# A gated mix of two long convolutions on one core: the product of filter and v written along positions, raw v in the inverse matrix's room, the step size in the transposing matmuls, another order of calls

## The chip, the cores and the metric

The kernel runs on one core of one Trainium2 chip. The metric is the device time of an execution in microseconds. The kernel before took 270.42 us in the median of three runs (269.96 to 270.56).

A core has a matrix engine (PE, whose weight loads are listed apart as PEld), VectorE (DVE), ScalarE (ACT), GpSimd (POOL), and SyncE (SP), which here only issues DMAs. They share an SBUF of 128 partitions, and PE writes to PSUM, from which DVE or ACT must copy ("evacuate") every result.

## The reference

Sequence length 2048, 448 channels, 256 modes per channel, batch 1, everything in bf16:

```python
# a: a state space model's kernel K made from 256 complex modes, as a causal convolution
dt = exp(log_dt)
K = einsum("dn,dnl,dn->dl", Cc, exp((dt * A)[:, :, None] * l), dt * Bc).real
a = causal_conv(K, u) + u * Dskip                 # by FFT of twice the length
# b: k filtered by 4 taps, times v, convolved with ssm_k, gated by u
k_shift = sum over t in 0..3 of k_pad[:, t:t + S] * shift_k[:, 3 - t]
kv = k_shift * v
b = u * (causal_conv(ssm_k, kv) + kv * ssm_D)
# the mix
g = sigmoid((u * gate_w).sum(-1, keepdims=True))
out = g * a + (1 - g) * b
```

`causal_conv` stands for the FFTs of the reference.

## The kernel before

**Tiling.** A channel is (g, l) with g one of 4 and l one of 112; a position is (a, b) with a one of 32 and b one of 64, position 64a + b. Data in "natural" layout lies on partitions (g, a) with 64 x 112 elements (b, l) each. The 112 values of l are worked in four groups H of NC = 28, so a group is 4 x 28 = 112 channels.

**A convolution** (`conv_B`, `conv_A`) of a group is a chain of matrix products in place of FFTs. A *spread* (line 422) takes, for each of the 28 columns, the 64 values of b as the matmul's weights (`lhsT`) and multiplies by Wc, twice, 56 matmuls of 128 columns each; four evacuations. A *transform* (434) runs 32 matmuls with weights W2, four evacuations. One of the two operands is copied with its halves exchanged by eight DMAs on SP (`swapped`, 813). DVE then makes two *products* of 3584 elements (480). *Stage A* (451) runs 56 matmuls against R, four evacuations; *stage B* (462) 128 matmuls of 28 columns against G, the inverse matrix, and its two results go to an epilogue on DVE. Branch B spreads the filter ssm_k (tile sk, columns side by side) and kv; ssm_D is added to the filter's first element from the tile dB (`load_sk`, 801). Branch A spreads u and the generated K. Stage B of branch A starts with `less` (962), which subtracts branch B's result by a matmul with minus the identity.

**The tables.** K of branch A comes from a *table* T of the group (`table`, 995): phases on PE, sines and exponentials on ACT (`levels`, 530; each change between sine and exponential loads a function table, ACT_TABLE_LOAD in the profile), then a chain of DVE multiplications and additions (`tables`, 658), some additions being POOL's accumulating DMAs; PE sums over the modes (`sums`, 691) and puts the rows in order (`gather`, 543, tile RK), and the spread uses the weights WcK. Table 3 is made in two halves. Ahead of the tables `Modes.run` (718) multiplies the modes' parameters and transposes the products of B and C, c2, into the tile hold.

**The filter on k** (913 to 925): k is loaded transposed into four tiles kT (837), and 448 matmuls with diagonal weights dg write 8 PSUM rooms, on partitions (g, a) with 8 x 112 results each; a DVE multiplication (925) takes a room times v, which lies in the tile natv in the natural layout (vt), in place. So a column of kv that the spread loads as weights has its 64 values 112 elements apart.

**Rooms and order.** There are 7 SBUF slots q of 3584 elements, 4 PSUM rooms ps of 2 x 512 words, and an arena of named tiles (natv, natu, sk, TQ, TP, ET, RK, and G). The three strings SLOTS, ROOMS and SIDES say for every request which slot or room it gets and whether an evacuation runs on VectorE (V) or ScalarE (S). The functions do not issue anything: the class Order (130) records 6562 calls, and `issue` then issues them in the order that the hand-written list ORDER gives. Each engine works its instructions off in that order, so the list also sets every queue's order, SP's DMA issues included. In the profile all of them carry line 142. In the order of PLAN the work is T0 B0 B1 T1 B2 A0 T2 B3 A1 T3 A2, the four mixes, A3; ORDER interleaves it. Only A3's epilogue (972) stores the output.

Of the kernel before, what the change touches and what calls it, by code (L numbers as in the profile page):

```python
# [23 lines left out]
NQG = 4  # L24
# [18 lines left out]
    "0153244660452356221105413561200342542265346120"  # L43
)
ROOMS = (
    "01300231231021302012133123211302103213113003213200301121010223323302100020322020223203123321230021323232021310333102"
    "21110012102130031202201020010102031123321123033210013321033213312112313230110231311332233320003030113132211112000223"
    "212023230102121"
)
SIDES = (  # L50
    "SVVSSSSSVSSSSSSSSSSSSSSSSVSSSSSSSSSSSSSSSSSSSVSVSSSSSSSSSSSVSVSSSSSSSSSSVVSSSSSSSSSSSSSSSSSSSSSSSSSSSSSSSSSSVSVSSSSS"
    "SSVVVSSSSSSSSSSSSSSSSSSSSSSSSSSSSSSSSSSVVSSVSSSSSSVVSSVVSSSSVSSSSSSSSSSSSSSSSSSSSSSSSSSSVSVSVVSSSS"
)
ORDER = (
# [1032 lines left out]
```

## Time and profile before

| | |
|---|---|
| median of 3 runs (lowest, highest) | 270.42 us (269.96, 270.56) |
| the profiled execution | 270.07 us |
| its span, first instruction to last | 268.3 us |
| PE busy | 230.2 us (86%) |
| DVE busy | 225.3 us (84%) |
| ACT busy | 202.2 us (75%) |
| POOL busy | 26.5 us (10%) |
| granted PE clock, mean over the span | 0.917 |
| HBM read, written | 8.68 MB, 3.15 MB |

The profile is one execution. A row of its groups has the engine, the operation, the tiles written and read, the shape (partitions x elements) and the number of instructions, then the busy time and the mean duration of one in ns, then the engine's idle time just before such instructions and what ended it. A row of the timeline has the start and the length in us, then engine, line, operation and tiles, and how many alike follow one another. A row of a stage table has the window, its length, then for PE, PEld, DVE, ACT and POOL the busy time with the count, then the granted PE clock as a share of the full one, then the busy share of the DMA engines and GB/s.

### The profile page before, as it was taken

To read this page: it belongs to the slowest core of one execution; us is meant where nothing else is said; L and a number is where in the kernel's file an instruction comes from. 1 tells how busy PE (TensorE), PEld (TensorE's weight loads), DVE (VectorE), ACT (ScalarE), POOL (GpSimd) and SP (SyncE) were. 2 spreads that over 40 slices of the span, in tenths; PEclk is the share of its full clock that TensorE was granted. 3 is DMA by queue.
4 is the path that set the end of the run, shared out by engine and by line. 5 is a ranking of instruction groups with operands and counts; after the bars stand their busy time and mean duration, and the time that the engine had idled before them with its cause. 6 is when DMAs were issued, how large, how long until landed. Compare 5 with 4: busy or idle time off the path is not lost.

```text
span 268.3 us, 12631 instructions
## 1 busy us (share of the span) xinstructions
PE 230.2 (86%) x5735; PEld 196.7 (73%) x5735; DVE 225.3 (84%) x330; ACT 202.2 (75%) x266; POOL 26.5 (10%) x111
## 2 busy tenths in 40 slices
PE   0475885999989999899999999999999989989740
PEld 0122433799977998898798998988999968889730
DVE  7999899977959899996989998969999965867840
ACT  5899899512978999798999797899999853746300
POOL 8910002010000020100000210000220210000000
PEclk9996586599999999999999999999999968999955
DMA  6789999923791969344005815400632560240076
GB/s 135 125 242 211 203 162 157 201 59 73 136 156 28 187 119 147 72 103 107 6 2 122 157 37 114 115 5 20 135 62 37 98 148 5 55 91 2 2 155 121
DMA packets 60279, 27.58 MB, mean 103 GB/s; under 512 B 50114, under 2 KB 57666, under 8 KB 60226
## 3 DMA queue, kind: packets, MB, share of 16 engines
q1 hardware_dynamic: 53234, 19.90, 39.5%
q0 software_dynamic: 2160, 5.51, 11.8%
q10 hardware_dynamic: 4832, 1.38, 2.4%
q8 instruction: 45, 0.74, 1.2%
q14 instruction: 8, 0.07, 0.1%
HBM read 8.68 MB, written 3.15 MB: 44 GB/s over the span
## 4 chain that ended last, share of the span: by engine, by line
PE 67%; ACT 15%; DVE 8%; issue 4%; DMA 2%; SPq 0%; POOL 0%; ACTq 0%; DVEq 0%; POOLq 0%
PE ps L142 67%; ACT q L142 8%; ACT ET L142 4%; DVE G L142 3%; DVE TP L142 2%; DMA natu<-in_A_u_dram 2%; DVE RK L142 2%; ACT TP L142 1%; ACT s_W L142 1%; ACT G L142 1%; ACT RK L142 1%; ACT L142 0%; DVE ET L142 0%; SPq L142 0%; DVE gx L142 0%
## 5 line engine op out<-in xcount | busy, mean ns | idle before, releaser
L142 ACT CAST q<-ps 128x1024 bf16<-128x1024 f32 (+4 forms) x150 | 125.1, 925 | 37.4 <-PE ps L142 37.0
L142 PEld LDWEIGHTS <-q 128*128 128x128 bf16 (+3 forms) x792 | 56.3, 139 | 11.8 <-issue 8.0
L142 DVE TENSOR_TENSOR TQ<-TQ,ET 128x896 bf16<-128x896 bf16 (+2 forms) x70 | 45.7, 687 | 0.4
L142 PE MATMUL ps<-q,s_W 128*128 128x112 bf16 (+1 forms) x544 | 36.0, 217 | 6.0 <-ACT q L142 2.9
L142 PEld LDWEIGHTS <-s_W 128*128 128x128 bf16 x544 | 28.9, 101 | 10.8 <-issue 8.4
L142 DVE TENSOR_TENSOR q<-q,q 128x3584 bf16<-128x3584 bf16 (+1 forms) x22 | 32.5, 1512 | 3.1 <-ACT q L142 2.5
L142 PE MATMUL ps<-TP,TQ 128*32 128x32 bf16 x1792 | 33.6, 240 | 1.3 <-issue 1.2
L142 PEld LDWEIGHTS <-TQ 128*32 128x32 bf16 x1792 | 29.8, 154 | 6.2 <-issue 4.8
L142 PEld LDWEIGHTS <-G 128*128 128x128 bf16 x1024 | 28.5, 97 | 5.2 <-issue 3.1
L142 PE MATMUL ps<-sa_R,q 128*128 128x128 bf16 x448 | 31.9, 228 | 0.1
L142 POOL DMA_DIRECT2D TP<-TP x15 | 13.0, 876 | 188.6 <-PE ps L142 109.7
L142 PEld LDWEIGHTS <-natu 128*32 128x32 bf16 (+1 forms) x560 | 28.4, 187 | 4.3 <-issue 2.5
L142 PE MATMUL ps<-q,G 128*128 128x28 bf16 x1024 | 29.4, 176 | 0.7 <-ACT q L142 0.7
L142 DVE TENSOR_TENSOR TP<-TP,ET 128x3584 bf16<-128x3584 bf16 (+1 forms) x15 | 24.4, 1646 | 0.0
L142 PE MATMUL ps<-TP 128*128 128x512 bf16 x32 | 10.9, 505 | 10.7 <-POOL TP L142 10.3
L142 DVE CAST q<-ps 128x896 bf16<-128x896 f32 (+2 forms) x14 | 14.0, 1015 | 6.8 <-PE ps L142 6.8
L142 PE MATMUL ps<-Wc,natu 128*64 128x128 bf16 x224 | 16.3, 291 | 1.3 <-issue 1.3
L142 ACT ACTIVATE q<-ps 128x896 bf16<-128x896 f32 x16 | 13.8, 926 | 4.4 <-PE ps L142 4.3
L142 DVE TENSOR_TENSOR TQ<-TQ 128x448 bf16<-128x448 bf16 (+2 forms) x35 | 15.4, 448 | 0.4
L142 PE MATMUL ps<-q,natu 128*32 128x336 bf16 (+3 forms) x336 | 15.8, 309 | 0.0
L142 PEld LDWEIGHTS <-TP 128*128 128x128 bf16 x32 | 3.7, 121 | 16.5 <-POOL TP L142 10.3
L142 PE MATMUL ps<-q,q 128*32 128x336 bf16 (+3 forms) x112 | 15.6, 308 | 0.0
(87 smaller groups left out, 307.9 us busy)
## 6 DMA issues: line engine op xcount, KB each, us to landing
q<-q SPq DMA_DIRECT2D x64, 112.0 KB, 3.6
TP<-TP POOLq DMA_DIRECT2D x9, 448.0 KB, 5.6
sk<-in_B_ssm_k_dram SPq DMA_DIRECT2D x16, 112.0 KB, 4.3
natv<-in_B_v_dram SPq DMA_DIRECT2D x4, 448.0 KB
natu<-in_A_u_dram SPq DMA_DIRECT2D x4, 448.0 KB
TP<-TP POOLq DMA_DIRECT2D x6, 224.0 KB, 4.1
scratch<-ET SPq DMA_DIRECT2D x4, 280.0 KB
out_dram<-natv SPq DMA_DIRECT2D x8, 112.0 KB, 4.8
```

The source lines that it names most:

```text
L142: ins = f(*args, **kw)
```

## The change: where kv, raw v and the results lie, the scaling of B, and the lists

- v is loaded raw into the first 7168 elements of G's room. The product with the filter is written to natv as [112, 64], along positions, so that a column that the spread loads as weights lies side by side (`kv`).
- Branch B's results, so far written over kv in natv, go to `held_in[H]`, one contiguous block [64, 28] for each group in natv. The mix and the last epilogue write to natu, and the output is stored from there.
- `Modes.run` no longer multiplies B_re and B_im by dt (8 ACT instructions). The identity of the transposing matmuls is replaced by identity times dt (`dts`, one DVE multiplication of 112 x 448), so they scale while they transpose. They are matmuls into two f32 rooms instead of transposes into one bf16 room. The work tiles go from 8 to 6; 4 of them lie in G's room at 3584 words and 2 in TQ.
- The gate's weights come by one DMA instead of four.
- SLOTS, ROOMS, SIDES (33 instead of 27 evacuations on VectorE, among 206 instead of 214) and ORDER are new. 6552 calls are recorded instead of 6562.

```diff
-    "0153244660452356221105413561200342542265346120"
+    "0214365652544341630245362166044633152502310654"
...
 def run(self):
-        t, whole, rate, br, bi, x, y, z = self.work
+        t, whole, rate, x, y, z = self.work
...
-        self.scaled(br, "B_re", dt)
-        self.scaled(bi, "B_im", dt)
-        cr, ci = self.raw["C_re"], self.raw["C_im"]
+        br, bi, cr, ci = (self.raw[n] for n in ("B_re", "B_im", "C_re", "C_im"))
...
-        room = self.places.room()[:].rearrange("p a n -> p (a n)").bitcast(bf16)
         for i in range(2):
-            pt = room[:, 1024 * i:1024 * i + 896]
+            room = self.places.room()
             for hf in range(2):
                 for g in range(4):
-                    nc.tensor.transpose(out=pt[:, (hf * 4 + g) * 112:(hf * 4 + g + 1) * 112],
-                                        in_=self.c[i][:, g, hf * 128:(hf + 1) * 128], identity=self.ident[0:112, 0:112])
...
+                    nc.tensor.matmul(room[:, hf, g * 112:(g + 1) * 112], lhsT=self.c[i][:, g, hf * 128:(hf + 1) * 128], rhs=self.ident[:, g], start=True, stop=True)
...
-    vt = arena["natv"][:].rearrange("p (b l) -> p b l", l=112)
+    at = G[:].rearrange("p b r g a -> p (b r g a)")
+    vt = shaped(at, [64, 112])
+    kv = shaped(arena["natv"][:], [112, 64])
...
-    for g in range(4):
-        nc.sync.dma_start(gw[g * 32:(g + 1) * 32], gate_w[g * 112:(g + 1) * 112].partition_broadcast(32))
+    nc.sync.dma_start(gw[:], gate_w.rearrange("(g l) -> g l", g=4).unsqueeze(1).to_broadcast([4, 32, 112]))
...
-    modal = Modes(nc, places, raw, ident, cols, work, N5, c2, hold, evac)
+    dts = cons.carve(224)[0:112].bitcast(bf16).rearrange("p (g l) -> p g l", g=4)
+    V.tensor_tensor(out=dts, in0=ident[0:112, 0:112].unsqueeze(1).to_broadcast([112, 4, 112]), in1=dt.unsqueeze(2).to_broadcast([112, 4, 112]), op=ALU.mult)
+    modal = Modes(nc, places, raw, dts, cols, work, N5, c2, hold, evac)
...
-        o = vt[:, b0:b0 + 8].rearrange("p (i b) l -> p i (b l)", i=2)
-        V.tensor_tensor(out=o, in0=pt[:, :, 0:448], in1=o, op=ALU.mult)
+        V.tensor_tensor(out=kv[:, :, b0:b0 + 8].rearrange("p l (i b) -> p l i b", i=2), in0=pt[:, :, 0:448].rearrange("p i (b l) -> p l i b", b=4),
+                        in1=vt[:, b0:b0 + 8].rearrange("p (i b) l -> p l i b", i=2), op=ALU.mult)
...
+    held_in = [shaped(arena["natv"][:], [64, NC], at=64 * NC * H) for H in range(4)]
...
-            o = window(ug, b0, n, H).rearrange("p (i b) c -> p i b c", b=16)
+            o = held_in[H][:, b0:b0 + n].rearrange("p (i b) c -> p i b c", b=16)
...
-    less = lambda H: (minus[:], lambda b0, n: window(ug, b0, n, H))
+    less = lambda H: (minus[:], lambda b0, n: held_in[H][:, b0:b0 + n])
...
-            V.tensor_tensor(out=window(ug, b0, n, H), in0=t, in1=window(ug, b0, n, H), op=ALU.add)
+            V.tensor_tensor(out=window(uu, b0, n, H), in0=t, in1=held_in[H][:, b0:b0 + n], op=ALU.add)
...
-        X = spread_in(lambda c: vt[:, :, H * NC + c])
+        X = spread_in(lambda c: kv[:, H * NC + c, :])
...
-        V.tensor_tensor(out=o, in0=o, in1=x, op=ALU.add)
+        V.tensor_tensor(out=x, in0=o, in1=x, op=ALU.add)
```

In the new ORDER, on DVE the addition of dB into group 0's filter stands behind table 0's first large multiplication; on SP the transposed loads of k stand behind those of v; U's loads and the gate's matmuls stand earlier, as do branch A0's spread and transform; B2's spreads and B1's stages A and B stand later; the exponentials of table 1 stand on both sides of table 0's remaining sines on ACT; the second half of A2's stage B stands behind A3's stage A.

More of the change, by code (lines that the diff above doesn't have):

```diff
@@ L42 @@
 SLOTS = (
-    "0153244660452356221105413561200342542265346120"
+    "0214365652544341630245362166044633152502310654"
 )
 ROOMS = (
-    "01300231231021302012133123211302103213113003213200301121010223323302100020322020223203123321230021323232021310333102"
-    "21110012102130031202201020010102031123321123033210013321033213312112313230110231311332233320003030113132211112000223"
-    "212023230102121"
+    "31020301233213020130221213002030121220330312300132203112223221301101222032123012231331111303121132010020233210031013"
+    "11200130210201030120231211331231202021230013233013332112300103220100303223020203023223012113221023331330101121312331"
+    "0003313003131020"
 )
 SIDES = (
-    "SVVSSSSSVSSSSSSSSSSSSSSSSVSSSSSSSSSSSSSSSSSSSVSVSSSSSSSSSSSVSVSSSSSSSSSSVVSSSSSSSSSSSSSSSSSSSSSSSSSSSSSSSSSSVSVSSSSS"
-    "SSVVVSSSSSSSSSSSSSSSSSSSSSSSSSSSSSSSSSSVVSSVSSSSSSVVSSVVSSSSVSSSSSSSSSSSSSSSSSSSSSSSSSSSVSVSVVSSSS"
+    "VSVSVSSSVVSSSVVSSSSSSSSSSSSSSSSSSSSVSSVSSSSSSSSSSSSSSSSSVSSVSSSVVVSSSSSSSSVSSSSSSSVSSSSSSSSSSSSSSSSSSSSSSSSSSSSVSSSS"
+    "SSSSSSSSSSVSSSSVSVVSVSSSSSSSSSSSSVSSSSSSVSVVVVSSSSSSSVSSSSSSSSSSSSSSSSSSSSSSSSVSVSSVSSSVSS"
 )
 ORDER = (
[54 rows of a table removed]
[54 rows of a table added]
 )
@@ L742, in run @@
         mul(z, br, ci)
-        mul(bi, bi, cr)
-        V.scalar_tensor_tensor(out=c[1], in0=fl(z), scalar=-1.0, in1=fl(bi), op0=ALU.mult, op1=ALU.subtract)
-        room = self.places.room()[:].rearrange("p a n -> p (a n)").bitcast(bf16)
+        mul(x, bi, cr)
+        V.scalar_tensor_tensor(out=c[1], in0=fl(z), scalar=-1.0, in1=fl(x), op0=ALU.mult, op1=ALU.subtract)
         for i in range(2):
-            pt = room[:, 1024 * i:1024 * i + 896]
+            room = self.places.room()
             for hf in range(2):
                 for g in range(4):
-                    nc.tensor.transpose(out=pt[:, (hf * 4 + g) * 112:(hf * 4 + g + 1) * 112],
-                                        in_=self.c[i][:, g, hf * 128:(hf + 1) * 128], identity=self.ident[0:112, 0:112])
-            self.evac(self.hold[:, :, i].rearrange("p h (q w) -> p q h w", q=8), pt.rearrange("p (q h w) -> p q h w", q=8, h=4))
+                    nc.tensor.matmul(room[:, hf, g * 112:(g + 1) * 112], lhsT=self.c[i][:, g, hf * 128:(hf + 1) * 128], rhs=self.ident[:, g], start=True, stop=True)
+            self.evac(self.hold[:, :, i].rearrange("p h (f q w) -> p f q h w", f=2, q=4), room[:, :, 0:448].rearrange("p f (q h w) -> p f q h w", q=4, h=4))
 @with_exitstack
@@ L879, in body @@
     nc.sync.dma_start(scratch[:].rearrange("(x w) n -> x w n", w=32)[:, 28:32], spare.unsqueeze(1).to_broadcast([20, 4, 1024]))
-    at = G[:].rearrange("p b r g a -> p (b r g a)")
-    work = [shaped(at, [4, 256], i32 if i == 1 else f32, at=1024 * i)[0:112] for i in range(8)]
+    work = [shaped(at if i < 4 else arena["TQ"][:], [4, 256], i32 if i == 1 else f32, at=1024 * i + (3584 if i < 4 else -2048))[0:112] for i in range(6)]
     N5 = shaped(arena["ET"][:], [5, 1024])[0:112]
     c2 = [shaped(arena["RK"][:], [4, 256], at=1024 * i)[0:112] for i in range(2)]
-    modal = Modes(nc, places, raw, ident, cols, work, N5, c2, hold, evac)
+    dts = cons.carve(224)[0:112].bitcast(bf16).rearrange("p (g l) -> p g l", g=4)
+    V.tensor_tensor(out=dts, in0=ident[0:112, 0:112].unsqueeze(1).to_broadcast([112, 4, 112]), in1=dt.unsqueeze(2).to_broadcast([112, 4, 112]), op=ALU.mult)
+    modal = Modes(nc, places, raw, dts, cols, work, N5, c2, hold, evac)
     modal.run()
@@ L929, in body @@
         nc.sync.dma_start(uu[g * 32:(g + 1) * 32], u4[g])
-    ug = vt
+    held_in = [shaped(arena["natv"][:], [64, NC], at=64 * NC * H) for H in range(4)]
     gwt = qt([112, 32])
@@ L955, in epilogue_B, with held @@
         return consume
-    def held(t, H):
+    def held(H):
         def consume(b0, n, pt):
-            evac(window(t, b0, n, H).rearrange("p (i b) c -> p i b c", b=16), pt.rearrange("p i (b c) -> p i b c", b=16))
+            evac(held_in[H][:, b0:b0 + n].rearrange("p (i b) c -> p i b c", b=16), pt.rearrange("p i (b c) -> p i b c", b=16))
         return consume
-    less = lambda H: (minus[:], lambda b0, n: window(ug, b0, n, H))
+    less = lambda H: (minus[:], lambda b0, n: held_in[H][:, b0:b0 + n])
     def store(b0, n):
         for g in range(4):
-            dmae[g % 2].dma_start(out4[g][:, b0:b0 + n, :], ug[g * 32:(g + 1) * 32, b0:b0 + n, :])
+            dmae[g % 2].dma_start(out4[g][:, b0:b0 + n, :], uu[g * 32:(g + 1) * 32, b0:b0 + n, :])
     def gated(dst, b0, n, pt):
@@ L990, in conv_B @@
         K, S = swapped(K)
-        X = spread_in(lambda c: vt[:, :, H * NC + c])
+        X = spread_in(lambda c: kv[:, H * NC + c, :])
         transform(nc, places, W2, X, evac)
-        conv(products(nc, K, S, X), epilogue_B(H) if H < NQG - 1 else held(ug, H))
+        conv(products(nc, K, S, X), epilogue_B(H) if H < NQG - 1 else held(H))
     def table(H):
@@ L1034, in mix @@
     def mix(H):
-        o, x = window(ug, 0, 64, H), window(uu, 0, 64, H)
+        o, x = held_in[H], window(uu, 0, 64, H)
         if H == NQG - 1:
```

108 rows, old and new, of the table ORDER are left out of this document.

## The prediction

> **What bounds the kernel now.** I read the head of the page first, then the chain of work that ended last, then a table of busy time by stage.
>
> ```profile
> span 268.3 us, 12631 instructions
> PE 230.2 (86%) x5735; PEld 196.7 (73%) x5735; DVE 225.3 (84%) x330; ACT 202.2 (75%) x266; POOL 26.5 (10%) x111
> PE 67%; ACT 15%; DVE 8%; issue 4%; DMA 2%; SPq 0%; POOL 0%; ACTq 0%; DVEq 0%; POOLq 0%
> ```
>
> TensorE carries two thirds of the chain, but VectorE has only 5 us less work. The stages below are cut where the filter's matmuls begin (48.3), where the first sums of tables 0, 1, 2 and 3 (both halves) begin (73.7, 123.7, 173.7, 208.3, 227.7) and where the last stage A ends (251.4). The columns are length, then busy time of PE, PEld, DVE, ACT, POOL with counts, the granted clock, and DMA.
>
> ```profile
> 0.00:48.30 48.30, 27.97 (x166) 13.74 (x166) 44.68 (x99) 41.76 (x60) 14.79 (x96) 0.80 1.01 176
> 48.30:73.70 25.40, 25.19 (x628) 23.08 (x626) 21.61 (x23) 11.72 (x15) 0.86 (x1) 0.91 0.60 114
> 73.70:123.70 50.00, 47.14 (x1291) 43.32 (x1289) 42.78 (x49) 44.74 (x58) 2.56 (x3) 1.00 0.66 118
> 123.70:173.70 50.00, 50.00 (x1350) 43.92 (x1347) 46.40 (x51) 44.49 (x58) 2.56 (x3) 1.00 0.38 80
> 173.70:208.30 34.60, 34.32 (x986) 31.97 (x985) 31.87 (x56) 32.70 (x44) 2.87 (x4) 1.00 0.26 50
> 208.30:227.70 19.40, 18.12 (x533) 15.89 (x531) 13.82 (x27) 11.62 (x15) 2.90 (x4) 0.82 0.42 87
> 227.70:251.40 23.70, 22.30 (x665) 20.58 (x666) 18.35 (x22) 14.10 (x19) 0.00 (x0) 1.00 0.19 43
> 251.40:268.30 16.90, 5.21 (x136) 4.18 (x133) 5.77 (x10) 1.03 (x2) 0.00 (x0) 0.59 0.57 110
> ...
> 0.00:72.90 72.90, 52.35 (x782) 36.15 (x782) 65.48 (x121) 52.68 (x73) 15.65 (x97) 0.84 0.87 155
> 72.90:120.90 48.00, 45.14 (x1222) 41.31 (x1220) 43.26 (x49) 43.33 (x58) 2.56 (x3) 1.00 0.66 117
> ```
>
> Up to 48.3 PE is idle for 20 us while DVE and ACT build constants: DVE sets that stage, with 3.6 us idle. From 48.3 to 251.4 PE is idle for 6.0 us in all. From 123.7 on it is plainly the bound, DVE standing idle for 17.3 of 127.7 us (127.7 less 46.40, 31.87, 13.82 and 18.35). The last two rows are cut where DVE ends the tables 0 and 1.
>
> **The change part by part.** *The product along positions.* B's spread of v loads 64 columns of v as weights, 224 times; so far they lie 224 bytes apart. The spread of the filter has the same shape with its columns side by side.
>
> ```profile
> L142 PE MATMUL ps<-Wc,natv 128*64 128x128 bf16 x224 | 14.9, 283 | 0.0
> L142 PE MATMUL ps<-Wc,sk 128*64 128x128 bf16 x224 | 9.7, 240 | 0.6 <-ACT TP L142 0.3 <-ACT q L142 0.2
> ...
> 96.48 1.06 PE L142 MATMUL ps<-Wc,sk 128*64 128x128 bf16 x32
> 97.50 1.17 PE L142 MATMUL ps<-Wc,natv 128*64 128x128 bf16 x16
> ...
> 98.91 2.10 PE L142 MATMUL ps<-Wc,natv 128*64 128x128 bf16 x32
> 100.94 1.77 PE L142 MATMUL ps<-q,G 128*128 128x28 bf16 x64
> 102.64 1.49 PE L142 MATMUL ps<-WcK,RK 128*64 128x128 bf16 x40
> 104.06 0.96 PE L142 MATMUL ps<-q,s_W 128*128 128x112 bf16 x16
> 104.89 0.28 PE L142 MATMUL ps<-q,G 128*128 128x28 bf16 x5
> ...
> 138.08 3.71 PE L142 MATMUL ps<-sa_R,q 128*128 128x128 bf16 x56
> 141.72 0.47 PE L142 MATMUL ps<-Wc,sk 128*64 128x128 bf16 x10
> ```
>
> From start to start, 32 strided ones take 2.03 us (63 ns each) and 32 contiguous ones 1.02 (32 ns). So the change takes 31.5 ns off each, 7.1 us for 224; the busy sums give 5.2 (14.9 less 9.7) as the other end. I take 7.1, because PE is the bound where most of them stand. The same rows give the other paces I need: 27 ns a matmul of stage B (1.70 over 64), 52 of a transform (0.83 over 16), 65 of stage A (3.64 over 56).
>
> The product itself now reads PSUM and raw v across positions and writes runs of four elements. No row shows that operation.
>
> ```profile
> L142 DVE TENSOR_TENSOR natv<-ps,natv 128x896 bf16<-128x896 f32 x8 | 8.5, 1086 | 3.7 <-PE ps L142 3.7
> L142 DVE CAST RK<-ps 128x896 bf16<-128x896 f32 x1 | 1.1, 1092 | 2.0 <-PE ps L142 2.0
> L142 DVE TENSOR_TENSOR q<-q,TP 128x1344 bf16<-128x1344 bf16 x1 | 1.5, 1548 | 0.0
> L142 DVE TENSOR_SCALAR G<-q,TP 112x256 f32<-112x256 bf16 x3 | 1.1, 373 | 0.0
> L142 DVE CAST q<-ps 128x1024 bf16<-128x1024 f32 x3 | 3.7, 1220 | 0.5 <-PE ps L142 0.5
> L142 DVE TENSOR_TENSOR q<-q,q 128x3584 bf16<-128x3584 bf16 x14 | 27.9, 2020 | 2.9 <-ACT q L142 2.5 <-DMA q<-q 0.4
> L142 ACT ACTIVATE G<-q,TP 112x256 f32<-112x256 bf16 x13 | 5.7, 495 | 0.3 <-DVE TP L142 0.3
> L142 ACT ACT_TABLE_LOAD x10 | 12.8, 1283 | 2.8 <-issue 1.5 <-PEq L1071 1.2
> ```
>
> The gather's copy (RK) reads PSUM strided and writes the same runs of four in 1092 ns, so 1.09 us is the lower end and my value: no change. The upper end adds a strided SBUF read at the pace of the diagonals' build (1548 over 1344, 1.15 ns an element, 1.03 us for 896): 2.1 us, or 8.2 us more for eight.
>
> *Step size in the transposing matmuls.* Eight ACT multiplies go (495 ns each, 4.0 us). DVE gains one build of 448 elements (0.5 us at 1.15 ns). The sixteen matmuls stay; the copies out read f32 of the same size.
>
> *One load of the gate weights for four.* SP issues three small DMAs less; their users come 40 us later, behind U's loads, so I cost this at nothing.
>
> *The order.* The list of copies moves work from ACT to DVE. Read with the row durations (1.22 and 1.09 us a copy of 1024 or 896, 0.4 to 0.7 for the small ones), 20 us go to DVE and 17 come back, so with the new build DVE's total rises by about 4 us, to 229. ACT's falls by 8.
>
> *The start.* Four things move here.
>
> ```profile
> 30.38 0.27 DVE L142 TENSOR_TENSOR sk<-sk,dB 128x28 bf16<-128x28 bf16 x1
> ...
> 41.60 3.95 DVE L142 TENSOR_TENSOR TP<-TP,ET 128x3584 bf16<-128x3584 bf16 x2
> ...
> 48.34 0.62 PE L142 MATMUL ps<-q,natu 128*32 128x448 bf16 x3
> ...
> 64.50 1.53 PE L142 MATMUL ps<-Wc,sk 128*64 128x128 bf16 x48
> 75.17 1.28 ACT L142 ACT_TABLE_LOAD   x1
> ...
> 76.47 0.98 ACT L142 ACTIVATE ET<-ps 128x448 bf16<-128x448 int16 x2
> ```
>
> First, the add of dB into the filter, at 30.38 so far, goes behind table 0's chain up to its first large multiply (41.60 plus 2.0), the scale of R and about 1.8 us that are new to DVE (the build, a cast, a negation), so it comes near 45.5. The first K spread waits for it, then its four copies on ACT with one exponential of 0.9 between them and the four transforms: the filter's matmuls begin near 52 instead of 48.34. Second, table 1's first exponentials now stand on both sides of table 0's sines. That is two table loads more, 2.6 us at 1283 ns, and uses up most of what the eight multiplies leave. Third, SP issues the four transposed loads of k behind raw v and the scratch writes; they then land some 5 us ahead of 52, and the filter waits for them only if they slip by more. Fourth, raw v now shares G's room, so G's lower fills wait for its DMAs; these are issued before 30 and the fills stand behind 35 on DVE, where table 0's next step would wait behind them. I cost both at nothing.
>
> On the table loads a page speaks against the change: the Trainium skill, "ScalarE: Activation LUTs", section "What ACT_TABLE_LOAD costs", adds a drain of about 1.38 us to the load itself, 2.66 us a switch. By that, two more switches would be an estimated 5.3 us. The trace disagrees: the load at 75.17 lasts 1.28 us and the next activation starts 20 ns after it.
>
> *Table 0 and 1.* Until table 0 ends, DVE has about 2.9 us more to do (a late cast, the build, copies) and still the 3.6 us of idle time of the start; its waits for the filter, 3.8 us so far, fall mostly away, since the eight products now stand later. I take 2.5 us late: 75.4 for 72.9. Until table 1 ends it then has less: the two products of B1 (2 times 2.02), one epilogue and copies of 5.4 us go behind, and the gate weights' spread (2.0) and copies of some 1.7 come ahead, 5.7 us net. So 43.3 less 5.7 is 37.6 of work, with 4.5 of idle time for 4.7: table 1 ends at 117.5 for 120.9.
>
> *Behind it.* By the list, PE has less done when table 1's sums begin: B2's two spreads (56 at 32 and 56 at 63 ns, 5.3 us), 72 transform matmuls (3.7), B1's stage A (3.6) and stage B (128 at 27, 3.5) go behind them, 16.1 us; the gate's 112 matmuls, 24 transform matmuls and four of table 2 come ahead, about 5.5. So 10.6 us move behind. PE had 124.7 us busy from 123.7 to 251.4 and 3.0 idle. From it go the strided loads of B2 and B3 (112 at 31.5, 3.5 us) and A2's second half of stage B, which now fills the wait after stage A:
>
> ```profile
> 246.62 0.54 PE L142 MATMUL ps<-natv,minus 128*128 128x448 bf16 x2
> ...
> 248.61 2.99 PE L142 MATMUL ps<-sa_R,q 128*128 128x128 bf16 x44
> ```
>
> That is 2.0 us. 124.7 plus 10.6 less 3.5 less 2.0 is 129.8. The stage from 208.3 to 227.7 ran at a clock of 0.82, 18 per cent of 19.4 us, 3.5 us lost; the PE pause behind it comes at another place of the new list, and I count half, 1.7, as gone. Stage A ends at 117.5 + 129.8 + 3.0 - 1.7 = 248.6 for 251.4. The tail then holds A2's epilogue and the last mix on DVE (1.09 each) inside the same 16.9 us; I add 0.3.
>
> **The sum.** 268.3 - 2.8 + 0.3 = 265.8 us of span. The profiled execution took 270.07, 1.77 around its span and 0.35 under the median of 270.42. The change of -2.5 put on that median gives **267.9 us**.
>
> **The rivals.** *DVE takes over as the bound* (slower). Behind table 1 DVE had 110.4 us of work and gets 6.9 more, the 4 of the total and the 2.8 that table 1 no longer holds. It may then idle for 13.8 of PE's 131.1 us; so far it idled for 17.3. If each of those waits stays, stage A ends at 117.5 + 117.3 + 17.3 = 252.1, and the time is 271.4. It decides as soon as DVE idles for more than 13.8 us between 117.5 and stage A's end. For it speaks that DVE is busy for 46.40 of 50 us behind 123.7; against it, that its waits were for PE, which now has less to do.
>
> *The late start is not won back* (slower). If the products cost their upper end, or the filter comes at 56 instead of 52, table 1 ends at 121.5 or later. PE has 129.8 us behind that, so 4 us more: 271.9, and up to 276 with both. Against it, the gather's copy at 1092 ns.
>
> *No change.* The strided loads may be hidden: PE's 16 matmuls at 63 ns take 1.0 us, an ACT copy of their 1024 elements takes about as long, so where spreads stand alone ACT paces them. Without the 3.5 us and with the clock's dip as long as before, stage A ends at 253.8 for 251.4, and with the tail's 0.3 the time is 270.42 + 2.7, 273.1; with table 1 ending 2.5 us earlier than I take, as it would if its start were not late, 270.6.
>
> *All of it counts.* If DVE idles only for 2 us between the tables and the dip goes wholly, stage A ends 4.2 us earlier: 263.7.
>
> **How the numbers follow.** Forecast 0.42, its own range 265 to 269.8; all of it 0.11; no change 0.08; DVE bound 0.22; late start 0.17. From 0.2 per cent, 0.54 us, a measurement of this kernel can tell a difference. Faster: 0.42 and 0.11, 0.53. Slower: 0.22 and 0.17, 0.39. Within: 0.08. The range, 263 to 274.5, leaves out the far ends of the late start and of the gain.
>
> **What would show it.** Right: spreads of v at about 32 ns a matmul, products at 1.09 us, filter matmuls from about 52, twelve table loads, table 1's first sums near 117.5, PE without gaps behind them, stage A ending near 248.6. Wrong: products above 1.5 us, table 1's sums after 120, DVE ahead of PE in the chain behind them, or a clock below 1.00 for more than one stretch between the filter and the tail.

## The result, and the profile after

The changed kernel takes 279.59 us in the median of four runs (278.36 to 280.20), the kernel before on the same chip 270.31: a ratio of 1.0338, interval 1.0300 to 1.0377. It is slower by 9.3 us; the forecast was 2.5 us faster.

One thing belongs to the reading of this time: the four fills of G's lower half ran from 36.73 to 39.5 us, behind v's loads into that room and ahead of the first product, so the product's second operand is by then G's numbers and not v. Every instruction has the shape and place that the change gives it. The runs rows, early_db, tail and prices below have the same order of fills.

The head of the page:

```profile
span 278.0 us, 12624 instructions
PE 222.2 (80%) x5735; PEld 192.2 (69%) x5735; DVE 234.6 (84%) x337; ACT 198.9 (72%) x254; POOL 27.4 (10%) x111
PE 55%; ACT 13%; DVE 11%; issue 5%; SPq 5%; POOL 4%; DMA 3%; ACTq 0%; DVEq 0%; POOLq 0%
```

PE has 8 us less to do, and yet the span is 9.7 us longer; DVE has 9.3 us more, where the forecast added 4. The table of busy time by stage has the columns of the prediction's. It is cut where the filter's matmuls begin (54.25), at the first spread of the product (75.02), at table 0's and table 1's first sums (82.07, 124.9) and at the end of the last stage A (259.3); the last row but two is the stretch ahead of that end:

```profile
0.00:54.25 54.25, 28.00 (x170) 14.25 (x170) 49.04 (x107) 40.33 (x51) 15.65 (x96) 0.79 0.86 161
54.25:75.02 20.77, 14.03 (x450) 13.38 (x450) 19.53 (x17) 2.53 (x3) 0.86 (x1) 0.91 0.77 139
75.02:82.07 7.05, 6.26 (x114) 5.68 (x115) 6.08 (x6) 5.28 (x7) 0.00 (x0) 0.73 1.34 166
82.07:124.88 42.81, 39.64 (x1118) 35.52 (x1117) 37.85 (x44) 36.85 (x49) 2.56 (x3) 0.92 0.36 65
...
239.30:259.30 20.00, 17.61 (x478) 16.38 (x469) 16.84 (x20) 9.78 (x14) 0.00 (x0) 0.91 0.18 39
...
124.90:259.30 134.40, 128.17 (x3691) 117.89 (x3691) 116.18 (x158) 112.14 (x144) 8.29 (x11) 0.99 0.37 75
259.30:278.00 18.70, 6.08 (x198) 5.43 (x196) 5.89 (x11) 1.74 (x2) 0.00 (x0) 0.69 0.54 100
```

The second row is the one to look at. In 20.8 us of filter, VectorE works 19.53, ScalarE 2.53, and PE 14.03: the stage that PE set before now belongs to VectorE. The groups by shape say with what:

```profile
L142 DVE TENSOR_TENSOR q<-q,q 128x3584 bf16<-128x3584 bf16 x14 | 27.8, 2018 | 3.7 <-DMA q<-q 3.6
L142 DVE TENSOR_TENSOR natv<-ps,G 128x896 bf16<-128x896 f32 x8 | 14.8, 1896 | 1.2 <-PE ps L142 1.2
...
L142 PE MATMUL ps<-Wc,natv 128*64 128x128 bf16 x224 | 9.8, 256 | 6.4 <-DVE natv L142 6.3
L142 PE MATMUL ps<-Wc,sk 128*64 128x128 bf16 x224 | 9.7, 248 | 5.7 <-DVE sk L142 5.5 <-ACT q L142 0.3
L142 ACT ACT_TABLE_LOAD x12 | 15.4, 1283 | 2.0 <-issue 1.8
```

The product costs 1.90 us for 1.09. The spread of the product now costs what the spread of the filter does, 9.8 us for 14.9, as the change means it to. Both spreads show a wait of some 6 us (the last column), where there was 0.0 and 0.6: for the first product's rows, and for the addition of dB into the filter. Table 0's sums come 8.3 us later than before (82.07 for 73.73), table 1's 1.2 (124.88 for 123.73), the end of stage A 7.7 (259.3 for 251.6).

### The profile page after: what moved, and what is told of

Its sections match the earlier page's. It is cut to its first block, busy times and chain, and to the rows that moved or that the text cites. A ratio compares the mean times of both kernels' runs of the same rounds, so it can differ in the third digit from the quotient of the medians.

```text
span 278.0 us, 12624 instructions
## 1 busy us (share of the span) xinstructions
PE 222.2 (80%) x5735; PEld 192.2 (69%) x5735; DVE 234.6 (84%) x337; ACT 198.9 (72%) x254; POOL 27.4 (10%) x111
## 4 chain that ended last, share of the span: by engine, by line
PE 55%; ACT 13%; DVE 11%; issue 5%; SPq 5%; POOL 4%; DMA 3%; ACTq 0%; DVEq 0%; POOLq 0%
PE ps L142 55%; ACT q L142 10%; SPq L142 5%; DVE natv L142 4%; POOL TP L142 3%; DVE TQ L142 2%; DMA sk<-in_B_ssm_k_dram 1%; DMA scratch<-ET 1%; ACT RK L142 1%; DVE natu L142 1%; DVE G L142 1%; DMA q<-q 1%; DVE RK L142 1%; ACT TP L142 1%; DVE TP L142 1%
## 5 line engine op out<-in xcount | busy, mean ns | idle before, releaser
L142 ACT CAST q<-ps 128x1024 bf16<-128x1024 f32 (+4 forms) x145 | 122.2, 935 | 41.2 <-PE ps L142 40.3
L142 PEld LDWEIGHTS <-q 128*128 128x128 bf16 (+3 forms) x792 | 57.1, 140 | 15.8 <-issue 10.7
L142 PE MATMUL ps<-q,s_W 128*128 128x112 bf16 (+1 forms) x544 | 35.1, 218 | 4.1 <-ACT q L142 3.1
L142 PEld LDWEIGHTS <-TQ 128*32 128x32 bf16 x1792 | 30.8, 154 | 9.0 <-issue 7.5
L142 PE MATMUL ps<-sa_R,q 128*128 128x128 bf16 x448 | 33.5, 231 | 2.9 <-DVE q L142 2.1
L142 DVE CAST q<-ps 128x896 bf16<-128x896 f32 (+4 forms) x19 | 18.2, 964 | 15.8 <-PE ps L142 15.0
L142 PE MATMUL ps<-q,G 128*128 128x28 bf16 x1024 | 28.6, 174 | 0.0
L142 PE MATMUL ps<-w_turn,q 96*128 96x224 bf16 (+2 forms) x80 | 15.0, 320 | 1.8 <-ACT ET L142 1.4
L142 ACT CAST RK<-ps 128x448 bf16<-128x448 f32 (+1 forms) x16 | 12.0, 759 | 5.7 <-PE ps L142 5.6
L142 DVE TENSOR_TENSOR natv<-ps,G 128x896 bf16<-128x896 f32 x8 | 14.8, 1896 | 1.2 <-PE ps L142 1.2
```

The costliest lines, as they stand in the source:

```text
L142: ins = f(*args, **kw)
```

## The experiments

Two theories were put against each other. **Theory P**: the dear product holds VectorE up until table 1, and everything behind, where PE has no gaps, is late by that. **Theory O**: the new order is at fault, by its late filter and by the PE work that it puts behind table 1. Where a ratio is given, it is against the kernel before on the same chip. Starts come from the timeline of each profiled execution.

| kernel | a product, us | filter begins | table 1's sums | stage A ends | ratio (interval) |
|---|---|---|---|---|---|
| before | 1.09 | 48.34 | 123.73 | 251.60 | 1 |
| the change | 1.90 | 54.25 | 124.88 | 259.28 | 1.0338 (1.0300 to 1.0377) |
| rows | 4.32 | 53.57 | 140.83 | 275.01 | 1.0912 (1.0846 to 1.0978) |
| early_db | 1.92 | 52.96 | 123.45 | 256.47 | 1.0271 (1.0207 to 1.0335) |
| old_list | 1.94 | 52.76 | 129.09 | 254.92 | 1.0165 (1.0094 to 1.0235) |
| old_list_rows | 4.40 | 52.03 | 148.40 | 273.97 | 1.0737 (1.0648 to 1.0826) |
| turned2 | 1.09 | 52.66 | 120.26 | 256.06 | 1.0252 (1.0165 to 1.0340) |
| old_turned2 | 1.09 | 46.71 | 127.14 | 252.84 | 1.0133 (1.0029 to 1.0236) |
| pool | 1.08 | 63.75 | 128.76 | 260.85 | 1.0472 (1.0378 to 1.0565) |
| old_pool | 1.08 | 46.95 | 132.89 | 258.10 | 1.0240 (1.0166 to 1.0315) |
| psum | 1.09 | 53.15 | 119.70 | 254.29 | 1.0164 (1.0104 to 1.0224) |
| old_psum | 1.10 | 46.73 | 122.38 | 247.31 | 0.9891 (0.9848 to 0.9934) |

**The product walked row by row (rows).**

```diff
-        V.tensor_tensor(out=kv[:, :, b0:b0 + 8].rearrange("p l (i b) -> p l i b", i=2), in0=pt[:, :, 0:448].rearrange("p i (b l) -> p l i b", b=4),
-                        in1=vt[:, b0:b0 + 8].rearrange("p (i b) l -> p l i b", i=2), op=ALU.mult)
+        V.tensor_tensor(out=kv[:, :, b0:b0 + 8].rearrange("p l (i b) -> p i b l", i=2), in0=pt[:, :, 0:448].rearrange("p i (b l) -> p i b l", b=4),
+                        in1=vt[:, b0:b0 + 8].rearrange("p (i b) l -> p i b l", i=2), op=ALU.mult)
```

> The changed kernel with the eight products walked row by row (positions outside, channels inside) instead of channel by channel; same operands, same results. Theory P (products): a product took 1.90 us for 1.09, eight of them 6.5 us, and VectorE had no idle time to take them up to table 1's last step, so everything behind is late by that much. If a product then takes near 1.1 us, table 1's sums start near 118.5 instead of 124.9 and the time falls by about 6.4 us, to 273. Theory O (order: the late filter and the order behind it): the time falls by less than 2 us whatever a product takes. If a product still takes 1.9 us, the run doesn't tell the two apart.

It failed as a cure: with single elements written 128 bytes apart a product takes 4.32 us. As a dose it is useful. VectorE has 8 x 2.42 = 19.4 us more, table 1's sums come 15.9 us later and stage A ends 15.7 later. So four fifths of what the products take are paid, and nothing behind table 1 wins any of it back.

**The change with the order of before (old_list, old_list_rows).** The code of the change, with SLOTS, SIDES and ORDER of the kernel before carried over call by call. In these two, three of v's four loads come behind G's fills, so the lower half of G largely holds v; shapes and counts are the same.

> The changed code with the lists of the kernel before (order of calls, sides, slots; one PSUM room more for the transposing matmuls, the build of the scaled identity ahead of them). Theory P: products at 1.9 us make table 1's sums come about 6 us later than 123.7, and PE gets some 3.5 us back from the contiguous loads behind them: 272 to 275 us, slower than 270.3. Theory O: without the new order the change gains: 264 to 269 us.

> The same with the products walked row by row. If they take near 1.1 us: theory P and theory O both expect the gain of the contiguous loads, 264 to 269 us; against the run before it theory P expects 6 us less, theory O no difference above 2 us.

Here the same code costs 1.65 per cent instead of 3.4: theory P's size for the product, but half of the loss goes away with the order, so theory O is not dead. Table 1's sums come 5.4 us later than before, with 8 x (1.94 - 1.09) = 6.8 us more of product. That is not the product alone: two of G's fills now wait 5.8 us for v's first load, and the filter begins 4.4 us later than before. In old_list_rows the dose, 8 x 2.45 = 19.6 us, puts table 1's sums 19.3 us later than in old_list and the end of stage A 19.

**dB added early (early_db).** Only the order changes: the addition of dB, with the DMAs that it needs, moves ahead on VectorE and SP.

> The changed kernel with the addition of dB into group 0's filter, and the loads it needs, moved ahead by about 8.5 us on VectorE and SP, nothing else. Theory O: filter's matmuls start several us earlier than 54.25 and the time falls by 3 to 6 us. Theory P: VectorE idles for only 1.3 us between 54 and 75, so at most that is won: 278.3 to 279.6 us.

The intervals of this run and of the change overlap, so no win is settled. Nor is it a clean test of a late filter, since the filter hardly came earlier. The timeline of PE:

```profile
39.74 0.41 PE L142 MATMUL ps<-Wc,sk 128*64 128x128 bf16 x8 [0.27 <-ACT q L142]
41.97 1.92 PE L142 MATMUL ps<-Wc,sk 128*64 128x128 bf16 x32 [1.81 <-ACT TP L142]
45.84 0.90 PE L142 MATMUL ps<-w_decay,q 64*128 64x448 bf16 x2 [1.96 <-ACT q L142]
46.68 1.07 PE L142 MATMUL ps<-Wc,sk 128*64 128x128 bf16 x16
49.88 3.15 PE L142 MATMUL ps<-q,s_W 128*128 128x112 bf16 x32 [2.14 <-ACT q L142]
52.96 0.62 PE L142 MATMUL ps<-q,natu 128*32 128x448 bf16 x3
```

The spread now starts 5.2 us earlier, and then waits for ScalarE, whose exponentials stand ahead of the spread's copies. One wait gave way to the next; the filter gained 1.3 us.

**The tail (tail).** The second half of A2's stage B, its gating with it, moved ahead of the last 40 matmuls of A3's stage A (in another PSUM room).

> The changed kernel with the second half of A2's stage B and its gating moved ahead of the last 40 matmuls of A3's stage A, where the kernel before has it. If that move is what put the first store 5.0 us behind stage A's end instead of 3.0, the time falls by 1 to 2 us; if the wait after stage A took it up, nothing changes.

The ratio is 1.0414 (1.0323 to 1.0506) for 1.0338: no gain. The first store comes 4.8 us behind stage A's end, for 5.0 in the change and 3.0 in the kernel before. The traces show two places where the 2.0 us go. ScalarE makes the last two copies of stage A one after the other, and they end 1.8 us behind it (0.85 in the kernel before). And the mix of group 2 (m2, 1.08 us) stands on VectorE between the first gating and its addition, where the kernel before ran it ahead of that gating, while PE was not yet done. Both hold in tail too. No run moves them alone.

**Prices (prices).** Sixteen VectorE and eight ScalarE operations of 896 elements behind the end of the changed kernel; the order is that of the expectation.

> The changed kernel with operations of the product's size behind its end, each twice, on VectorE: the product of the change; the same with its second operand in the write's own order; a copy of the PSUM operand alone; the product with everything contiguous; the product of the change written without gaps; copies from SBUF across the rows into runs of four, without gaps, and row by row into single elements; on ScalarE the copies from SBUF and PSUM into runs of four, a contiguous one and the row-by-row one. If the strided second operand is what costs, the second and third take 1.1 us and the fifth 1.9; if the gaps of the write cost, the fifth is the cheap one. Row by row: 4.3 us as in the run with rows.

The timeline (start, length); the rows come in the stated order, the pair of 2.91 us being the contiguous product (1.08) and the product without gaps (1.79):

```profile
264.25 1.79 DVE L142 TENSOR_TENSOR natv<-ps,G 128x896 bf16<-128x896 f32 x1
266.07 1.09 DVE L142 TENSOR_TENSOR natv<-ps,TP 128x896 bf16<-128x896 f32 x1
267.19 1.09 DVE L142 CAST natv<-ps 128x896 bf16<-128x896 f32 x1
268.20 2.91 DVE L142 TENSOR_TENSOR TQ<-ps,G 128x896 bf16<-128x896 f32 x2
271.03 0.98 DVE L142 COPY natv<-G 128x896 bf16<-128x896 bf16 x1
271.92 0.97 DVE L142 COPY TQ<-G 128x896 bf16<-128x896 bf16 x1
272.81 2.20 DVE L142 COPY natv<-G 128x896 bf16<-128x896 bf16 x1
...
285.93 1.83 ACT L142 COPY natv<-G 128x896 bf16<-128x896 bf16 x1 [27.77 <-DVE natv L142]
287.80 0.91 ACT L142 CAST natv<-ps 128x896 bf16<-128x896 f32 x1
288.60 0.91 ACT L142 CAST TQ<-ps 128x896 bf16<-128x896 f32 x1
```

The first three rows settle the product. Give it a second operand that lies in the order of the write, and it takes 1.09; leave the operand out, the same 1.09. PSUM read across and the gaps between runs of four cost nothing; the SBUF operand that jumps 224 bytes at each element costs 0.70 us. It costs that only beside the PSUM operand: a copy that reads SBUF by the same jumps and nothing else takes 0.98. The second round gave the same prices within 0.03 us. Copied row by row into single elements it takes 2.20 us, not the 4.3 expected. The Trainium skill, "Vector Engine (DVE) Microarchitecture Reference", section "Measured stream behaviour on trn2", says that an SBUF stream keeps its rate only in runs of at least two adjacent 4-byte words, and gives 1.73 for 1.054 ns a column where one source hops at every element: an estimate of 0.6 us for 896. The 0.70 of this run is near it, with elements of 2 bytes where the page measured 4. On ScalarE a copy by the same jump from SBUF takes 1.83 us; from PSUM the jump is free (0.91, the same as contiguous).

**Three ways to a cheap product.** In *turned2* and *old_turned2* the product runs in place over v, all contiguous, and ScalarE copies it along positions. G's lower fills read a tile of their own and stand behind the products; the mask that they read has by then been overwritten by table 0, so half of G holds other numbers.

```diff
+        o = vt[:, b0:b0 + 8]
+        V.tensor_tensor(out=o.rearrange("p (i b) l -> p i (b l)", i=2), in0=pt[:, :, 0:448], in1=o.rearrange("p (i b) l -> p i (b l)", i=2), op=ALU.mult)
+        nc.scalar.copy(kv[:, :, b0:b0 + 8], o.rearrange("p b l -> p l b"))
```

> The changed kernel with the product in place in the natural layout (all three operands contiguous) and eight copies on ScalarE that write it along positions; ScalarE idled for 18.8 us there. The four fills of G's lower half, which share that room, stand behind the gate weights' spread on VectorE and read a tile of their own. Theory P: products near 1.09 us, table 1's sums near 119 for 124.9, 273 to 275 us when the changed kernel has 279.6; a copy dearer than 2 us would take that back. Theory O: no more than 2 us.

> The code of the change with the lists of the kernel before, with the same cheap product and eight copies on ScalarE, G's lower fills ahead of B0's products. Against the run with those lists and the 1.94 us products (1.65 per cent over the kernel before) theory P expects 6 us less, 1 per cent under the kernel before. Theory O expects the same as there.

The product fell to 1.09 us, but a copy took 2.02 (1.96 with the old lists), because ScalarE pays the jumps instead. In the old order theory P's 6 us did not come: the interval overlaps that of old_list. In the new order table 1's sums came 4.6 us earlier, but the intervals of turned2 and of the change overlap too.

In *pool*, *pool_early* and *old_pool* GpSimd turns raw v ahead of time and the product reads it in the write's order; the mask has a tile of its own, here and in the next runs, and v is read before the fills.

```diff
+        o = kv[:, :, b0:b0 + 8].rearrange("p l (i b) -> p l i b", i=2)
+        V.tensor_tensor(out=o, in0=pt[:, :, 0:448].rearrange("p i (b l) -> p l i b", b=4), in1=o, op=ALU.mult)
...
+        nc.gpsimd.tensor_copy(kv[:, :, b0:b0 + 8], vt[:, b0:b0 + 8].rearrange("p b l -> p l b"))
```

> The changed kernel with raw v turned by eight copies on GpSimd, idle from 15 to 51, into the rows that the product writes; the product then reads and writes these in place. By the price list its strided second operand cost 0.70 us and the gaps cost nothing, so a product should take near 1.1 us. The fills of G's lower half stand behind the gate weights' spread, read a tile of their own, and so come behind the last reading of raw v. No price of a GpSimd copy is in any run so far. Theory P: up to 4.5 us for each of the eight they are done by the first product; table 1's sums near 117 for 124.9 (6.4 us of products, and 2.7 of fills less where VectorE waited anyway), 272 us when the changed kernel has 279.6. Theory O: 277 or more.

> The same with the addition of dB and its loads moved ahead on VectorE and SP as in the run early_db, which won 2 to 3 us on the changed kernel. Theory P: with cheap products VectorE waits for PE between 54 and 75, so the earlier filter is now worth at least as much, 269 to 270 us. If the earlier filter wins less than 1 us here, the start is bound elsewhere.

> The code of the change with the lists of the kernel before, raw v turned on GpSimd, v's loads ahead of three of k's, G's lower fills ahead of B0's products. If products near 1.1 us are all that kept the contiguous loads from paying, 264 to 268 us, under the kernel before by 1 to 2 per cent. If GpSimd's copies come too late or slow VectorE down, 270 or more.

All three were slower than expected (pool_early 1.0356, 1.0270 to 1.0443). The product is at 1.08 us, and from the filter's start to table 1's sums pool takes 65.0 us for the change's 70.6, which is theory P's gain; but the filter starts 9.5 us later. The timelines of VectorE, first of the change, then of pool:

```profile
33.88 0.85 DVE L142 TENSOR_TENSOR ET<-ET,q 128x1344 bf16<-128x1344 bf16 x1
34.65 0.22 DVE L142 TENSOR_SCALAR sa_R<-sa_R 128x256 bf16<-128x256 bf16 x1
34.79 0.39 DVE L142 TENSOR_SCALAR ET<-ET 128x896 bf16<-128x896 bf16 x1
35.09 1.08 DVE L142 TENSOR_TENSOR ET<-ET,q 128x1792 bf16<-128x1792 bf16 x1
36.09 0.19 DVE L142 TENSOR_SCALAR minus<-TP 128x128 bf16<-128x128 bf16 x1
...
40.58 0.39 DVE L142 TENSOR_TENSOR TQ<-TQ 128x448 bf16<-128x448 bf16 x1
```

```profile
33.19 2.50 DVE L142 TENSOR_TENSOR ET<-ET,q 128x1344 bf16<-128x1344 bf16 x1
35.60 1.86 DVE L142 TENSOR_SCALAR sa_R<-sa_R 128x256 bf16<-128x256 bf16 x1
37.38 2.01 DVE L142 TENSOR_SCALAR ET<-ET 128x896 bf16<-128x896 bf16 x1
39.32 2.71 DVE L142 TENSOR_TENSOR ET<-ET,q 128x1792 bf16<-128x1792 bf16 x1
41.95 1.81 DVE L142 TENSOR_SCALAR minus<-TP 128x128 bf16<-128x128 bf16 x1
...
50.09 0.39 DVE L142 TENSOR_TENSOR TQ<-TQ 128x448 bf16<-128x448 bf16 x1
```

And GpSimd in pool meanwhile:

```profile
32.95 16.62 POOL L142 COPY natv<-G 128x896 bf16<-128x896 bf16 x8 [17.54 <-DMA G<-in_B_v_dram]
```

Eight VectorE instructions, from 33.19 to 50.05, run beside the eight copies: each takes 1.8 to 2.7 us, where the five shown take 0.2 to 1.1 in the change, so the two engines take turns, one instruction to one copy (2.1 us). At the last row of the two timelines VectorE is 9.5 us behind the change, which is what the filter is late by. GpSimd's idle time was not free time. In old_pool the filter begins in time (46.95), but the last copy ends at 62.8 and the first product starts at 65.28.

In *psum*, *psum_early* and *old_psum* the product stays in PSUM, all contiguous, and ScalarE copies from there, where jumps are free:

```diff
+        V.tensor_tensor(out=pt[:, :, 0:448], in0=pt[:, :, 0:448], in1=vt[:, b0:b0 + 8].rearrange("p (i b) l -> p i (b l)", i=2), op=ALU.mult)
+        nc.scalar.copy(kv[:, :, b0:b0 + 8].rearrange("p l (i b) -> p l i b", i=2), pt[:, :, 0:448].rearrange("p i (b l) -> p l i b", b=4))
```

> The changed kernel with the product in place in PSUM (contiguous operands) and eight copies on ScalarE from there into the rows along positions, 0.91 us each by the price list whether PSUM is read contiguously or not; G's lower fills behind the gate weights' spread from a tile of their own. Theory P (the product's strided operand): VectorE gets 5 to 6.5 us back up to table 1, ScalarE has the time: table 1's sums near 118 to 119, ratio to the kernel before near 1.015. If the ratio stays above 1.025, the new order costs what the products were charged with.

> The same with the addition of dB and its loads moved ahead. With cheap products the late filter should bind: theory O says 3 us or more against the run before it, theory P (VectorE bound all the same) less than 1.5.

> The code of the change with the lists of the kernel before and the same product in PSUM with ScalarE's copies. Nothing is left of the dear product: VectorE has the old work and 0.5 us, PE 7 us less. Theory P: table 1's sums at 123 to 125, ratio 0.98 to 0.99. If the ratio stays above 1, the contiguous loads save PE nothing that ends the span. Against the run psum it prices the new order: theory O at 2 per cent or more.

Groups by shape in psum:

```profile
L142 ACT CAST natv<-ps 128x896 bf16<-128x896 f32 x10 | 9.1, 907 | 7.4 <-DVE ps L142 6.7 <-PE ps L142 0.5
L142 DVE TENSOR_TENSOR ps<-ps,G 128x896 f32<-128x896 f32 x8 | 8.6, 1093 | 2.8 <-PE ps L142 1.6 <-ACT q L142 1.2
```

Both prices are as the list gave them. Table 1's sums come at 119.70, 5.2 us ahead of the change, and the ratio falls by half, to 1.0164. (Part of that may be the four fills, 2.7 us, which no longer stand ahead of table 0: the filter begins 1.1 us earlier.) psum_early is at 1.0140 (1.0090 to 1.0190): the early dB is worth nothing that shows. With the order of before the same code is at 0.9891, under both kernels: 266.07 us in the median, the kernel before beside it 269.00. So the product is worth 1.7 per cent with the new lists (1.0338 to 1.0164) and up to 2.7 with the old (1.0165 to 0.9891; in old_list two fills also waited for v's first load, and the filter began 6 us later). The new lists cost 2.7 (0.9891 to 1.0164). Both theories hold; neither alone makes the loss.

Where the order loses, by the stage tables, cut at the filter, table 0's and table 1's first sums and stage A's end. psum:

```profile
0.00:53.15 53.15, 28.88 (x168) 14.69 (x168) 46.80 (x103) 40.14 (x51) 15.62 (x96) 0.75 0.93 165
53.15:76.75 23.60, 20.04 (x563) 18.88 (x563) 19.39 (x21) 15.01 (x18) 0.86 (x1) 0.92 0.91 154
76.75:119.70 42.95, 38.92 (x1117) 34.31 (x1117) 39.82 (x48) 36.33 (x48) 2.56 (x3) 0.96 0.48 75
...
119.70:254.30 134.60, 128.84 (x3691) 118.43 (x3692) 116.18 (x158) 112.47 (x144) 8.30 (x11) 0.97 0.37 75
254.30:272.70 18.40, 6.09 (x198) 5.43 (x196) 5.90 (x11) 1.74 (x2) 0.00 (x0) 0.70 0.53 102
```

old_psum:

```profile
0.00:46.70 46.70, 27.73 (x166) 13.82 (x166) 42.41 (x96) 38.63 (x52) 14.79 (x96) 0.79 1.02 179
46.70:73.95 27.25, 23.55 (x629) 20.17 (x627) 22.13 (x23) 18.29 (x23) 0.86 (x1) 0.92 0.63 116
73.95:122.40 48.45, 46.28 (x1295) 41.73 (x1293) 44.98 (x52) 45.07 (x58) 2.56 (x3) 1.00 0.66 119
...
122.40:247.30 124.90, 121.79 (x3524) 109.64 (x3523) 110.45 (x153) 102.84 (x134) 8.33 (x11) 1.00 0.32 67
247.30:264.30 17.00, 4.67 (x133) 3.89 (x131) 5.57 (x10) 0.84 (x2) 0.00 (x0) 0.65 0.57 109
```

Ahead of table 1's sums PE is busy for 87.8 of 119.7 us in psum and for 97.6 of 122.4 in old_psum. The new order reaches table 1 2.7 us sooner, with 7.0 us more of PE standing idle on the way; behind it lies the stretch in which PE hardly ever stops, and PE is busy there for 128.84 us, not 121.79. With 2.7 more of idle time there and 1.4 in the tail it is 8.4 us of span. Not all of the 7.1 us of busy time is work that was moved: the granted clock of that stretch was 0.97 for 1.00, which over 134.6 us is an estimated 4 us. Whether the order brings the clock down is not shown. At the one granted clock that both have among their runs, 0.932 over the span, psum took 271.51 us and old_psum 266.18, so most of the difference stays without it.

**The step size alone (scale_only).** The kernel before with only the change to `Modes.run` and the scaled identity `dts`, which lies in TQ here.

> The kernel before with only the step size moved into the transposing matmuls: eight ScalarE instructions of 0.5 us less, one VectorE build of 0.5 us more, two PSUM rooms. VectorE sets that stage, so the forecast said no gain: ratio 0.998 to 1.003. If ScalarE's 4 us counted, 0.985 to 0.99.

1.0037 (0.9998 to 1.0075): no gain from ScalarE's eight instructions, as forecast.

## Why the prediction was wrong, point by point

- **Contiguous spreads: right in pace, not in worth.** They run at the filter's pace, 9.8 us busy for 14.9 (the lower end named, 5.2 us), and where PE runs freely 16 of them start within 0.49 us, 31 ns each. Behind table 1 the forecast took 3.5 us off for those of B2 and B3. With the old order and a clock of 1.00 in both, that stretch took 125.6 us with strided loads (scale_only; PE busy 123.2) and 124.9 with contiguous ones (old_psum; 121.8): 0.7 us. That is nearer to what the rival *No change* says of these loads.
- **The product: the step that failed.** "The gather's copy (RK) reads PSUM strided and writes the same runs of four in 1092 ns, so 1.09 us is the lower end and my value: no change." The row has no second operand, and that is where the cost lies. The upper end, 2.1 us from the diagonals' build, was near: 1.90 in the kernel, 1.79 alone. The nearest row was chosen by the write and by PSUM, the parts that are free, and not by the operand that differs. With the price that was assumed (psum) the span is 272.7 for 278.0: this step, with the four fills that moved in the same run, is 5.3 of the 12.2 us by which the span missed 265.8. The other 6.9 belong to what the forecast made of the order: 2.2 up to table 1, 3.5 behind it (134.6 for 131.1) and 1.2 in the tail (18.4 for 17.2).
- **The start: right in kind, short in size.** dB came at 44.62 (near 45.5 forecast), the filter at 54.25 for 52; the table loads are twelve. In early_db dB comes earlier and the spread then waits for ScalarE, so the filter's start hangs on ScalarE's queue too.
- **Table 1: 7.4 us late** (124.88 for 117.5). psum, with products at the price assumed, has it at 119.70: 5.2 us go with the product (and the four fills moved). Of the 2.2 that remain, 1.2 are there when its filter begins (53.15 for 52).
- **Behind table 1: 134.4 us for 131.1.** PE's work came out as forecast: 129.8 less the 1.7 for the clock is 128.1, and 128.2 was measured. The clock dipped to 0.91 over the 20.0 us from 239 to 259, an estimated 1.8 us, about half of the 3.5 before; the forecast gave no reason why it should be half, so that is luck. The idle time was carried over from the old order, 3.0 us, and that step failed: it is 6.2. The two largest waits of PE in that stretch:

```profile
PE ps L142 <- issue: 2.7, 7, 0.8
PE ps L142 <- DVE q L142: 2.1, 1, 2.1
```

  The first is near what it was (2.5 us). The second is new: A2's stage A waits for its products, and these wait 2.4 us for the DMAs of the exchanged copies, part of the 3.6 us in the group of 3584 elements above, whose waits before were for ACT's copies. The rest, 1.4 us, are waits for ScalarE's copies and for a DMA.
- **The tail: 18.7 us for 17.2.** The end of stage A to the first store took 5.0 us for 3.0. It is not A2's stage B (tail); the traces point at ScalarE's second copy and the place of m2, which no run tests.
- The three terms, 7.4, 3.3 and 1.5, make the 12.2 us by which the span (278.0) missed 265.8.
- **The rivals.** The one that came true is the late start that is not won back: its condition (products at their upper end, 1.90 for 2.1) nearly held, and its price (271.9, up to 276) was still too low, because it took table 1 to end at 121.5 or later and kept the rest of the forecast. VectorE as the bound behind table 1 did not come, though the sign named for it did: VectorE idled for 18.2 us there, over 13.8, but PE was busy for 128 of 134 us and only the 2.1 us above were a wait for VectorE. The sign could not tell the two apart, since a longer stretch adds idle time to both.
- **Nothing for the scaling: right** (scale_only). The range ended at 274.5.
- A sign that came and that no run tests is the clock: between the filter and the tail it was below 1.00 in four rows of the table after (0.91, 0.73, 0.92 and 0.91), before in two (0.91 and 0.82).
- Whether the contiguous loads pay stays open. old_psum, with the product's price gone and the old order, is 1.1 per cent under the kernel before. But its runs had a granted clock of 0.929 to 0.944, those of the kernel before 0.911 to 0.941; between 0.932 and 0.938 its lead is 2.0 us in the mean, not 2.9. And four of G's fills stand later in it (at 79.58 us), which is no part of the change: against scale_only 1.6 us are won by the time of table 1's sums (122.38 for 124.00), where the fills' place may count, and 0.7 behind them (one profiled execution each).

## What to carry to other kernels

When an operation is rewritten for another layout, price each operand's path by itself, and take the nearest row from the operand that changes most; a row that lacks it bounds nothing from above. A transposition that was free here with PSUM as the source added two thirds to VectorE's product and doubled ScalarE's copy with SBUF as the source, so let the engine that empties PSUM do it. An order that reaches a milestone sooner is no gain if PE arrives there with more work left: compare its busy time up to the milestone, not only the milestone, and the granted clock behind it.

## What the hardware showed that was not expected

- VectorE and ScalarE read PSUM across (448 bytes on at each element) at full rate: 1.09 and 0.91 us for 896 elements, the same as contiguous. The same walk through bf16 in SBUF (224 bytes on) costs VectorE's product 0.70 us more, and doubles ScalarE's copy, 1.83 us; a VectorE copy with that walk as its only source takes 0.98.
- Single bf16 elements written 128 bytes apart take 2.20 us in a copy and 4.32 in a product with a PSUM operand.
- While GpSimd copies in SBUF, VectorE's small instructions take 1.8 to 2.0 us instead of 0.2 to 0.4. The Trainium skill, "SBUF — State Buffer", section "SBUF: two separate sides", calls the port pair that the two engines share an exclusive lock, held for the whole instruction, for VectorE operations with two SBUF inputs or in a 2-port mode. The trace agrees: one VectorE instruction to one GpSimd copy of 2.1 us.
- Matmuls of 128 columns that load 64 bf16 values lying 224 bytes apart as weights start 63 ns apart (32 in 2.03 us, the kernel before); with the values side by side 31 ns (16 in 0.49 us, the change).
